# Attention scores computed a second time, keys by queries, in place of transposed probabilities

## The chip, the cores and the metric

The kernel runs on one core of one Trainium2 chip. A core has engines that run side by side, each with its own in-order stream of instructions: PE (TensorE, matmuls into PSUM), DVE (VectorE), ACT (ScalarE, activations and copies), POOL (GpSimd, which does not touch PSUM here) and SP (SyncE, which here only starts DMAs). The metric is the time of one execution on the device in microseconds (us), lower is better. The time before is the median of three runs.

## What is computed

One transformer block over 2048 tokens of width 1024, all in 32-bit floats: a LayerNorm, 32 heads of attention in four segments of 512 tokens with a memory carried from one segment to the next, an output projection with a residual, two LayerNorms, and an MLP of width 3584. The change lies in the softmax attention inside a segment. Cut to that (H = 32 heads, Dh = 32, L = 512):

```python
h = x + A(layernorm(x))                  # attention
h2 = h + B(layernorm(h))                 # MLP with its own LayerNorm
# inside A, for each segment s:
logits = einsum("bhqd,bhkd->bhqk", qs, ks) * Dh ** -0.5 + mask   # -1e9 above the diagonal
p = softmax(logits, axis=-1)
a_dot = einsum("bhqk,bhkd->bhqd", p, vs)
a_mem = (phi(qs) @ M) / (phi(qs) @ z + 1e-6)
o = g * a_mem + (1.0 - g) * a_dot        # g = sigmoid(beta), one value a head
```

## The kernel before, in words

Every 32-bit matrix is split into a high part that TensorE's fast 32-bit mode keeps exactly and a low rest, and a product is the sum of high by high, high by low and low by high.

The sequence is done in two halves of 1024 tokens. A half is: attention, output projection (`wo_first`, `wo_second`), LayerNorms, MLP. In attention eight groups `g` of four heads run over the half's two segments `sl`; one group and segment is a unit, so there are 32 units and 128 heads (one head of one segment counts as one head here).

`dense(g, sl, ...)` makes a unit's keys, queries and values: three projections (`kps`, `qps`, `vps`) of eight steps each, a step being three matmuls of 512 columns (`mm3`, lines 115 to 117). It builds the stacks: for each head, `ks` holds the key's high, low and high part in 96 rows, `qs` the query's high, high and low part, so that one 96-row product gives the exact score. Twelve DMAs a unit fill each kind of stack on SP's queue (line 377); a kind has five buffers. `vs` holds the values by tokens, high and low side by side (64 columns).

Heads of the unit before run between the projection steps of the unit that is projected. `slot` issues one head's work in six steps by the table `PLAN`; the head in its first pass is `cur`, the one before it `p1`, the one before that `p2`, so a head's work is spread over up to three slots. `interleave` takes one step of `heads` after each projection step, so a unit's 24 projection steps hold four slots. The plan's letters are: `q` score product of 128 queries by their keys with the row minimum of minus the score on DVE (line 542) and the exponential on ACT with the row sum (line 550); `n` normalization by sum and gate on POOL (line 557); `t` transposes of the probabilities on PE (line 573) and the cast to the high part on ACT (line 575); `s` the low part on DVE (line 580); `a` output products on PE (line 593), keys block by block; `o` the sum of the two value parts on DVE (line 604), the memory's part on POOL and the store or the split for the output projection.

Small matmuls of the memory (`one_small`) are slipped between the heads' matmuls. PSUM's eight banks are shared by tag: three for projections and small matmuls (`d`), two for scores (`qk`), two for transposes (`pt`), one for outputs (`av`).

The order in the program is only a priority. The framework plans when the kernel is built: it takes for each engine and queue the earliest instruction in the program's order that it expects to be ready, by its own estimates of durations, and puts in every wait. That plan is fixed: on the chip each engine then works in that order. Manual dependencies (`add_manual_dep`) force an order where they stand.

At the end of a half the last unit's heads run between the steps of `wo_first`, which multiplies the first segment's outputs; its steps for the last group wait for that group's output.

Of the kernel before, what the change touches and what calls it, by code (L numbers as in the profile page):

```python
# [17 lines left out]
P = 128  # L18
# [12 lines left out]
PLAN = ('q1 S2', 'q0 n0 a0', 'q2 t0 a1', 'q3 n2 s0 o', 't1', 's1 t2')  # L31
SCALE = DH ** -0.5
EPS = 1e-5
DEN_EPS = 1e-6
# [9 lines left out]
def build(tc, x, wq, wk, wv, wo, beta, w1, b1, w2, b2, out):  # L44
# [11 lines left out]
    hsel = const.tile([P, 76], F32, name="hsel")[:, 0:4]  # L56
# [11 lines left out]
    def constants():  # L68
# [3 lines left out]
        nc.scalar.activation(gate[:, 1, :], gate[:, 0, :], AF.Identity, scale=-1.0, bias=1.0)  # L72
        pb = ps_dense("pb")
# [5 lines left out]
    mz_dram = dram.tile([P, NG * 132 + 96], F32, name="mz_dram")  # L79
    o_dram = [dram.tile([NG, P, 512], F32, name=f"o_dram{s}") for s in range(4)]  # L80
# [251 lines left out]
    def attention_pool(half):  # L332
# [5 lines left out]
        acts["mz"] = ab.tile([P, NG * 132 + 96], F32, name="MZ")  # L338
        if half == 0:
            nc.gpsimd.memset(acts["mz"], 0.0)  # L340
        else:
            nc.sync.dma_start(acts["mz"], mz_dram)

    def attention(half, first):
# [27 lines left out]
        def stack(a, b, name, order):  # L372
            out = []
            for j in range(4):
                st = ab.tile([96, 512], F32R, tag=name, name=name, bufs=5)
# [5 lines left out]
        small = []  # L381

# [19 lines left out]
        def dense(g, sl, ws, u):  # L402
# [59 lines left out]
            vs = ab.tile([P, 16, 64], F32R, name="vs", bufs=2)  # L462
            u["vs"] = vs
# [66 lines left out]
        offs = [0, 128, 384, 768]  # L530
        koff = [0, 512, 1024, 896]

        def qk(st, i):
            u, j = st["u"], st["j"]
            if "pr" not in st:
                st["pr"] = ab.tile([P, 1280], F32, name="pr", bufs=2)
                st["mx"] = ab.tile([P, 32], F32, name="mx", bufs=4)
                st["nm"] = ab.tile([P, 32], F32, name="nm", bufs=4)
            n = P * (i + 1)
            pqk = psum.tile([P, 512], F32, tag="qk", name="pqk", bufs=2)  # L540
            nc.tensor.matmul(pqk[:, :n], u["qs"][j][:, i * P:(i + 1) * P], u["ks"][j][:, 0:n], start=True, stop=True)  # L541
            nc.vector.tensor_tensor_reduce(  # L542
                out=st["pr"][:, offs[i]:offs[i] + n], in0=pqk[:, :n], in1=mask[:, 512 - n:512],
                op0=ALU.add, op1=ALU.min, scale=-SCALE, scalar=3.0e38, accum_out=st["mx"][:, i:i + 1])
            soft(st, i)

        def soft(st, i):
            pr, mx = st["pr"], st["mx"]
            pi = pr[:, offs[i]:offs[i] + P * (i + 1)]
            nc.scalar.activation(pi, pi, AF.Exp, bias=mx[:, i:i + 1], scale=-1.0, accum_out=mx[:, 4 + i:5 + i])  # L550

        def norm(st, i):
            pr, mx, nm, j, g = st["pr"], st["mx"], st["nm"], st["j"], st["u"]["g"]
            nc.vector.reciprocal(nm[:, 4 + i:6 + i], mx[:, 4 + i:6 + i])  # L554
            for k in (i, i + 1):
                pi = pr[:, offs[k]:offs[k] + P * (k + 1)]
                nc.gpsimd.tensor_scalar(pi, pi, nm[:, 4 + k:5 + k], gate[:, 1, 4 * g + j:4 * g + j + 1],  # L557
                                        op0=ALU.mult, op1=ALU.mult)

        def ptr(st, n):  # L560
            grp = ((0,), (1, 3), (2,))[n]
            if n == 0:
                st["pth"] = ab.tile([P, 1280], F32R, name="pth", bufs=2)
                st["ptl"] = ab.tile([P, 1280], F32R, name="ptl", bufs=2)
            pr, pth, ptl = st["pr"], st["pth"], st["ptl"]
            ppt = psum.tile([P, 512], F32, tag="pt", name="ppt", bufs=2)
            base = koff[grp[0]]
            w = 0
            for jk in grp:
                for i in range(jk, 4):  # L570
                    one_small()
                    o = koff[jk] - base + (i - jk) * P
# [9 lines left out]
        def av(st, n):  # L582
            u, j = st["u"], st["j"]
            if n == 0:
                st["po"] = psum.tile([P, 512], F32, tag="av", name="po", bufs=1)[0:64, :]
# [858 lines left out]
```

## Time and profile before

| what | value |
|---|---|
| time, median of three runs | 2301.37 us (2301.26 to 2301.75) |
| span of the profiled execution | 2296.2 us |
| median of the runs minus that span | 5.2 us |
| PE busy | 2270.4 us, 99% of the span |
| DVE, ACT, POOL busy | 67%, 53%, 48% of the span |
| granted TensorE clock | 1.000 |
| attention with heads running, both halves | about 36 to 520 us and 920 to 1425 us |

The profiled execution has no time of its own in the runs; its span, from its first to its last instruction, is 5.2 us under the median of the runs, and that much lies around it.

How to read it: a group of instructions is given by source line, engine, operation, output and inputs; then its count, its busy time and the mean duration of one in ns; then how long the engine had been idle just before such instructions and what ended that idle time. Durations of matmuls overlap, so they do not add. `SPq` and `ACTq` are DMA issues on the queues of SP and ACT; what is issued from ACT's queue stands in ACT's own order.

### The profile page before, as it was taken

Reading aid. Unit: us, or ns where it says so; the run is one execution under the profiler, and the core shown is the slowest. Engines: PE = TensorE matmul, PEld = TensorE weight load, DVE = VectorE, ACT = ScalarE, POOL = GpSimd, SP = SyncE. Lnnn points to the kernel's source line nnn. Section 1 sums busy time; section 2 is a strip of 40 time slices with the busy share of each in tenths; the row PEclk is TensorE's granted clock in tenths of the full one; section 3 lists DMA queues with packets and bytes.
Section 4 is the critical chain, followed back from the end, with each engine's and each line's share of the span. In section 5 each row is a group of like instructions: output and inputs, shape, how many; then the busy total and the mean of one; then the engine's idle time right before and its main releaser. Section 6 shows DMA issues by size and latency. Waiting matters only on the chain.

```text
span 2296.2 us, 35279 instructions
## 1 busy us (share of the span) xinstructions
PE 2270.4 (99%) x11769; PEld 1890.8 (82%) x11769; DVE 1540.3 (67%) x3173; ACT 1225.0 (53%) x2549; POOL 1092.4 (48%) x1134
## 2 busy tenths in 40 slices
PE   8999999999999999999999999999999999999999
PEld 6888888878888888888888887888888888888887
DVE  6777777776655565777777777565566766577563
ACT  6777777775453445777777776363344223322221
POOL 5545555555244442555555556253445554155430
PEclk9999999999999999999999999999999999999999
DMA  6333333345465654433333344466667976476762
GB/s 190 92 85 91 93 89 85 87 120 182 139 204 172 188 165 142 113 91 86 85 87 88 87 111 140 156 211 175 176 188 263 345 243 216 159 253 221 249 234 90
DMA packets 322719, 355.36 MB, mean 155 GB/s; under 512 B 26190, under 2 KB 218730, under 8 KB 322538
## 3 DMA queue, kind: packets, MB, share of 16 engines
q1 hardware_dynamic: 259370, 316.40, 45.4%
q10 hardware_dynamic: 63168, 36.71, 5.3%
q8 instruction: 93, 1.52, 0.3%
q14 instruction: 88, 0.72, 0.1%
HBM read 226.59 MB, written 76.09 MB: 132 GB/s over the span
## 4 chain that ended last, share of the span: by engine, by line
PE 91%; ACT 3%; POOL 2%; DVE 2%; issue 1%; DMA 1%; ACTq 0%; SPq 0%; POOLq 0%; DVEq 0%
PE po L1278 22%; PE bps L882 9%; PE cps L882 7%; PE dps L882 6%; PE po L593 6%; PE ppt L573 6%; PE pqk L541 3%; PE vps L116 2%; PE vps L115 2%; PE kps L115 2%; PE kps L116 2%; PE vps L117 2%; PE kps L117 2%; PE pwo L117 2%; PE pwo L116 2%; PE pwo L115 2%
## 5 line engine op out<-in xcount | busy, mean ns | idle before, releaser
L557 POOL TENSOR_SCALAR pr<-pr,nm,gate 128x128 f32<-128x128 f32 (+3 forms) x512 | 322.6, 639 | 345.9 <-DVE nm L554 260.0
L550 ACT ACTIVATE pr<-pr,mx 128x256 f32<-128x256 f32 (+3 forms) x512 | 287.6, 562 | 161.9 <-DVE mx L542 158.2
L580 DVE TENSOR_TENSOR ptl<-ppt,pth 128x512 fp32r<-128x512 f32 (+1 forms) x384 | 227.2, 599 | 86.2 <-ACT pth L575 82.0
L542 DVE CUSTOM_DVE_ANT_0 pr<-pqk,mask 128x256 f32<-128x256 f32 (+3 forms) x512 | 243.3, 484 | 46.5 <-PE pqk L541 43.7
L573 PE MATMUL ppt<-ident,pr 128*128 128x128 f32 x1280 | 223.6, 277 | 2.1 <-POOL pr L557 1.4
L575 ACT CAST pth<-ppt 128x512 fp32r<-128x512 f32 (+1 forms) x384 | 194.2, 517 | 39.0 <-PE ppt L573 33.1
L1288 DVE TENSOR_TENSOR c<-c,po 128x512 f32<-128x512 f32 x160 | 105.4, 683 | 143.1 <-PE po L1278 135.5
L573 PEld LDWEIGHTS ppt<-ident,pr 128*128 128x128 f32 x1280 | 164.6, 140 | 32.5 <-POOL pr L557 2.6
L541 PE MATMUL pqk<-ks,qs 96*128 96x256 f32 (+3 forms) x512 | 161.3, 315 | 0.0
L92 POOL TENSOR_TENSOR wl<-wr,wh 128x1024 fp32r<-128x1024 f32 x52 | 124.5, 2393 | 70.8 <-PE pqk L541 27.6
L593 PE MATMUL po<-pth,vs 128*64 128x512 f32 (+3 forms) x512 | 155.4, 326 | 0.3 <-ACT pth L575 0.2
L593 PE MATMUL po<-ptl,vs 128*64 128x512 f32 (+3 forms) x512 | 153.9, 310 | 1.3 <-DVE ptl L580 1.2
L1278 PE MATMUL po<-w2h,zh 128*128 128x512 f32 x378 | 121.1, 390 | 0.8 <-DVE zh L1218 0.4
L1135 POOL TENSOR_TENSOR w2r<-w2r 128x512 f32<-128x512 f32 x54 | 85.4, 1593 | 72.0 <-DVE c L1288 36.9
L541 PEld LDWEIGHTS pqk<-ks,qs 96*128 96x128 f32 x512 | 96.2, 188 | 21.5
L994 POOL TENSOR_TENSOR s<-r 128x512 f32<-128x512 f32 x28 | 43.6, 1559 | 143.4 <-DVE sa L1010 87.1
L882 PE MATMUL bps<-zh,sb 128*128 128x512 f32 x336 | 111.0, 391 | 0.0
L882 PE MATMUL bps<-zh,sa 128*128 128x512 f32 x336 | 110.8, 390 | 0.0
L115 PE MATMUL vps<-yh,wh 128*128 128x512 f32 x256 | 109.4, 427 | 0.9 <-DVE MZ L497 0.9
L115 PE MATMUL kps<-yh,wh 128*128 128x512 f32 (+1 forms) x264 | 110.1, 417 | 0.0
L115 PE MATMUL qps<-yh,wh 128*128 128x512 f32 x256 | 106.8, 417 | 0.0
L1278 PE MATMUL po<-w2h,hl 128*128 128x512 f32 x322 | 103.2, 390 | 0.5 <-POOL hl L1218 0.3
(241 smaller groups left out, 6657.1 us busy)
## 6 DMA issues: line engine op xcount, KB each, us to landing
hr<-h_dram SPq DMA_DIRECT2D x112, 448.0 KB, 5.4
w2r<-in_B_w SPq DMA_DIRECT2D x122, 256.0 KB, 4.4
r<-in_B_w SPq DMA_DIRECT2D x56, 512.0 KB, 4.5
h_dram<-ht ACTq DMA_DIRECT2D x84, 256.0 KB, 3.7
ks<-kh SPq DMA_DIRECT2D x256, 64.0 KB, 2.0
qs<-qh SPq DMA_DIRECT2D x256, 64.0 KB, 2.0
wr<-in_A_wo SPq DMA_DIRECT2D x32, 512.0 KB, 4.0
wx<-in_B_w SPq DMA_DIRECT2D x56, 256.0 KB, 3.5
```

Of the source, the lines that this page charges most:

```text
L115: nc.tensor.matmul(ps, ah, bh, start=first, stop=False)
L116: nc.tensor.matmul(ps, ah, bl, start=False, stop=False)
L541: nc.tensor.matmul(pqk[:, :n], u["qs"][j][:, i * P:(i + 1) * P], u["ks"][j][:, 0:n], start=True, stop=True)
L542: nc.vector.tensor_tensor_reduce(out=st["pr"][:, offs[i]:offs[i] + n], in0=pqk[:, :n], in1=mask[:, 512 - n:512], op0=ALU.add, op1=ALU.min, ...
L550: nc.scalar.activation(pi, pi, AF.Exp, bias=mx[:, i:i + 1], scale=-1.0, accum_out=mx[:, 4 + i:5 + i])
L557: nc.gpsimd.tensor_scalar(pi, pi, nm[:, 4 + k:5 + k], gate[:, 1, 4 * g + j:4 * g + j + 1], op0=ALU.mult, op1=ALU.mult)
L573: nc.tensor.transpose(ppt[:, o:o + P], pr[:, offs[i] + jk * P:offs[i] + (jk + 1) * P], ident)
L575: acts["pth"] = n, nc.scalar.copy(pth[:, base:base + w], ppt[:, :w])
L580: nc.vector.tensor_tensor(o, x0, x1, op=ALU.subtract)
L593: nc.tensor.matmul(po[:, P * jk:], v, st[part][:, koff[jk]:koff[jk] + w], start=(jk, part) == (0, "pth"), stop=(jk, part) == (2, "ptl"))
L882: nc.tensor.matmul(ps, x_[:, c, :], y_[:, c, :], start=first and c == 0 and n == 0, stop=last and c == 3 and n == 2, skip_group_check=True)
L1278: nc.tensor.matmul(ps, x_[:, k], y_[k], start=opens and k == 0 and i == 0, stop=closes and k == self.KP - 1 and i == 2, skip_group_check=True)
```

## The change

The transposes of the probabilities, their normalization before the output product and the sums of the exponential go. In their place:

- The row minimum of minus the unscaled score still comes from the first score product (`qk`); the masked scores are written back into PSUM and not used further.
- `halves` splits the minima of a head's four query blocks into a high and a low part on POOL; `rows` turns these eight columns into rows with one transpose, copies them to SBUF on ACT and sends them with two DMAs on ACT's queue into rows 96 and 97 of the head's query stack. The key stacks hold ones in these rows, set once in eight buffers that are used in turn. The query stacks keep their five buffers.
- `turned` multiplies key blocks by queries over 98 rows, so the product is the score minus its row maximum, already with keys on the partitions; ACT takes the exponential, POOL clears the triangle above the diagonal.
- `cast` makes the high part on ACT and the low part on DVE (on POOL for the third group).
- The values get a column of ones (column 64), so that row 64 of the output product holds the sums (`av`, 65 rows).
- `av_out` sends the sum row of each head by DMA into 32 partitions; after the fourth head it takes reciprocals, multiplies by one minus the gate, stores the weights to DRAM, loads them back spread over 32 partitions a head, and multiplies the output.
- `PLAN` becomes the table below; small matmuls are slipped in at nine places a head, not at seventeen. The unit's output tile moves to the pool of LayerNorm tiles, and the loads of `x` for the first output blocks are ordered behind one of the output copies.

```diff
-PLAN = ('q1 S2', 'q0 n0 a0', 'q2 t0 a1', 'q3 n2 s0 o', 't1', 's1 t2')
+PLAN = ('q1 r c1', 'q2 c2', 'q0 a0', 'q3 a1 b0', 'b1 a2', 'b2 m c0 o')
...
+        acts["ks"] = [ab.tile([98, 512], F32R, name=f"ks{i}") for i in range(KB)]
+        acts["vs"] = [ab.tile([P, 16, 72], F32R, name=f"vs{i}") for i in range(2)]
+        for t in acts["ks"]:
+            nc.gpsimd.memset(raw(t[96:98, :]), 1.0)
+        for t in acts["vs"]:
+            nc.gpsimd.memset(raw(t[:, :, 64:65]), 1.0)
...
             nc.vector.tensor_tensor_reduce(
-                out=st["pr"][:, offs[i]:offs[i] + n], in0=pqk[:, :n], in1=mask[:, 512 - n:512],
-                op0=ALU.add, op1=ALU.min, scale=-SCALE, scalar=3.0e38, accum_out=st["mx"][:, i:i + 1])
-            soft(st, i)
...
+                out=pqk[:, :n], in0=pqk[:, :n], in1=mask[:, 512 - n:512],
+                op0=ALU.add, op1=ALU.min, scale=-1.0, scalar=3.0e38, accum_out=st["mx"][:, i:i + 1])
+
+        def halves(st):
+            mm = st["mm"] = ab.tile([P, 32], F32R, name="mm", bufs=2)
+            nc.gpsimd.tensor_copy(mm[:, 0:4], st["mx"][:, 0:4])
+            nc.gpsimd.tensor_tensor(mm[:, 4:8], st["mx"][:, 0:4], raw(mm[:, 0:4]), op=ALU.subtract)
+
+        def rows(st):
+            pm = psum.tile([P, 512], F32, tag="pt", name="pmr", bufs=2)
+            one_small()
+            nc.tensor.transpose(pm[0:8, 0:P], raw(st["mm"][:, 0:8]), ident)
+            mr = ab.tile([P, P], F32, name="mr", bufs=1)[0:8, :]
+            nc.scalar.copy(mr, pm[0:8, 0:P])
+            q = st["u"]["qs"][st["j"]]
+            for r in range(2):
+                nc.scalar.dma_start(raw(q[96 + r:97 + r, :]), mr[4 * r:4 * r + 4, :])
+
+        def turned(st, n):
...
+            for jk in groups[n]:
+                c = P * (4 - jk)
+                w += c
+                nc.tensor.matmul(ps[:, koff[jk]:koff[jk] + c], u["ks"][j][:, jk * P:(jk + 1) * P], u["qs"][j][:, jk * P:],
+                                 start=True, stop=True)
+            pe = st["pe", n] = ab.tile([P, 512], F32, tag="pe", name="pe", bufs=3)
+            nc.scalar.activation(pe[:, :w], ps[:, :w], AF.Exp, scale=SCALE)
+            d = pe[:, 0:P * len(groups[n])].rearrange("p (a b) -> p a b", b=P)
+            nc.gpsimd.affine_select(d, d, pattern=[[0, len(groups[n])], [1, P]], compare_op=ALU.is_ge, fill=0.0, base=0,
+                                    channel_multiplier=-1)
+
+        def cast(st, n):
...
+            acts["pth"] = n, nc.scalar.copy(st["pth", n][:, :w], pe)
+            (nc.gpsimd if n == 2 else nc.vector).tensor_tensor(st["ptl", n][:, :w], pe, raw(st["pth", n][:, :w]),
+                                                              op=ALU.subtract)
...
+            nc.scalar.copy(sm[32 * j:32 * j + 1, :], po[64:65, :])
+            nc.sync.dma_start(rq[b, :], sm[32 * j:32 * j + 1, :])
+            op = nc.scalar.copy(ot[b, :], po[32:64, :])
...
             if j == 3:
+                g = u["g"]
+                nc.vector.reciprocal(rq, rq)
+                nc.gpsimd.tensor_scalar(rq, rq, gatec[:, g:g + 1], None, op0=ALU.mult)
+                rd = r_dram[turns["v"] % 2]
+                nc.sync.dma_start(rd.rearrange("j (e n) -> (j e) n", n=16), rq)
+                rr = u["rr"]
+                for k in range(4):
+                    nc.sync.dma_start(rr[32 * k:32 * k + 32, :], rd[k:k + 1, :].to_broadcast([32, 512]))
+                nc.gpsimd.tensor_tensor(ot, ot, rr, op=ALU.mult)
...
-            ops = {"q": (cur, qk), "n": (cur, norm), "N": (p1, norm), "t": (p1, ptr), "s": (p1, sub), "S": (p2, sub),
-                   "a": (p2, av), "o": (p2, av_out)}
+            ops = {"q": (cur, qk), "m": (cur, halves), "r": (p1, rows), "b": (p1, turned), "c0": (p1, cast),
+                   "c": (p2, cast), "a": (p2, av), "o": (p2, av_out)}
...
-            nc.sync.dma_start(hts[t], x[0, r0:r0 + P, :])
+            op = nc.sync.dma_start(hts[t], x[0, r0:r0 + P, :])
+            if sl == 0:
+                tc.add_manual_dep(op.ins, acts["ot"].ins.name, NOSYNC, reason="program order")
```

More of the change, by code (lines that the diff above doesn't have):

```diff
@@ L545, in qk @@
-            soft(st, i)
[L547 to L567, printed above, removed]
-            w = 0
[L569 to L572, printed above, removed]
-                    nc.tensor.transpose(ppt[:, o:o + P], pr[:, offs[i] + jk * P:offs[i] + (jk + 1) * P], ident)
-                    w += P
-            acts["pth"] = n, nc.scalar.copy(pth[:, base:base + w], ppt[:, :w])
-            st["sub", n] = (ptl[:, base:base + w], ppt[:, :w], raw(pth[:, base:base + w]))
```

77 lines of the change are left out of this document (48 added, 29 removed).

## The prediction

> **What bounds the kernel now.** I read the page first, then two stretches of the attention by engine, then the order of time inside one head.
>
> ```profile
> span 2296.2 us, 35279 instructions
> ...
> PE 2270.4 (99%) x11769; PEld 1890.8 (82%) x11769; DVE 1540.3 (67%) x3173; ACT 1225.0 (53%) x2549; POOL 1092.4 (48%) x1134
> ...
> PE 91%; ACT 3%; POOL 2%; DVE 2%; issue 1%; DMA 1%; ACTq 0%; SPq 0%; POOLq 0%; DVEq 0%
> ```
> ```profile
> 1000.00:1300.00 300.00, 300.00 (x1838) 254.37 (x1837) 226.81 (x678) 219.93 (x559) 167.39 (x226) 1.00 0.34 87
> ```
> ```profile
> L573 PE MATMUL ppt<-ident,pr 128*128 128x128 f32 x390 | 68.0, 277 | 0.0
> ```
>
> The first fence is the page (span, engines, the chain that ended last); the second a stretch of attention by engine (PE, PEld, DVE, ACT, POOL, granted clock); the third one group in that stretch. PE carries 91% of the chain and is busy for all 300 us, at full clock; DVE stands at 76%, ACT at 73%, POOL at 56%. The 390 transposes are 10 a head, so 39 heads in 300 us: 7.69 us a head, of which a head's own steps are only part, since projections run between them. Busy time doesn't price a matmul, because durations overlap; the distance from one start to the next does.
>
> ```profile
> 401.53 0.22 PE L541 MATMUL pqk<-ks,qs 96*128 96x128 f32 x1
> 401.59 0.39 PE L593 MATMUL po<-pth,vs 128*64 128x512 f32 x1
> ...
> 403.09 0.34 PE L541 MATMUL pqk<-ks,qs 96*128 96x384 f32 x1
> 403.27 0.60 PE L573 MATMUL ppt<-ident,pr 128*128 128x128 f32 x4
> 403.62 0.30 PE L593 MATMUL po<-pth,vs 128*64 128x128 f32 x1
> 403.77 0.23 PE L593 MATMUL po<-ptl,vs 128*64 128x128 f32 x1
> ...
> 404.76 0.39 PE L541 MATMUL pqk<-ks,qs 96*128 96x512 f32 x1
> 404.99 0.40 PE L115 MATMUL vps<-yh,wh 128*128 128x512 f32 x1
> 405.22 0.40 PE L116 MATMUL vps<-yl,wh 128*128 128x512 f32 x1
> ...
> 405.69 0.60 PE L573 MATMUL ppt<-ident,pr 128*128 128x128 f32 x4
> 406.04 0.48 PE L115 MATMUL vps<-yh,wh 128*128 128x512 f32 x1
> 406.36 0.40 PE L116 MATMUL vps<-yl,wh 128*128 128x512 f32 x1
> ```
>
> Here a score product of 512 columns holds PE 0.23 us (404.76 to 404.99), of 384 0.18, of 128 0.06; 256 are taken as half of 512, 0.12. A product over 128 rows holds it as long (404.99 to 405.22), so 98 rows in place of 96 cost nothing. Four transposes and the product behind them take 405.69 to 406.36, 0.67; less that product's 0.23 it is 0.44, or 0.11 a transpose.
>
> **The change on PE, a head.** Removed: 10 transposes, 1.10 us. Added: four products by keys, 0.23 + 0.18 + 0.12 + 0.06 = 0.59; one transpose of the eight columns of maxima, 0.11; and a small exposed load where the 128-column product stands ahead of a small output product: between 0 and the 0.09 by which 403.62 to 403.77 exceeds 0.06, taken as 0.04. The 65th output row changes no column count. Net 1.10 - 0.74 = 0.36 us a head; the 1280 transposes of the page are 128 heads: **46 us off PE**.
>
> **The other engines.** They cost nothing while they stay below PE, which is their cover; without it, these loads would show.
>
> ```profile
> L557 POOL TENSOR_SCALAR pr<-pr,nm,gate 128x128 f32<-128x128 f32 (+3 forms) x512 | 322.6, 639 | 345.9 <-DVE nm L554 260.0
> L550 ACT ACTIVATE pr<-pr,mx 128x256 f32<-128x256 f32 (+3 forms) x512 | 287.6, 562 | 161.9 <-DVE mx L542 158.2
> ...
> L575 ACT CAST pth<-ppt 128x512 fp32r<-128x512 f32 (+1 forms) x384 | 194.2, 517 | 39.0 <-PE ppt L573 33.1
> ```
> ```profile
> L550 ACT ACTIVATION_READ_ACCUMULATOR pr<-pr,mx 128x1 f32 x512 | 96.4, 188 | 0.0
> ...
> L575 ACT CAST pth<-ppt 128x256 fp32r<-128x256 f32 x128 | 49.2, 385 | 10.1 <-PE ppt L573 10.0
> ...
> L363 ACT ACTIVATE e<-qps 128x512 f32<-128x512 f32 x24 | 14.6, 607 | 1.5 <-DVE ql L428 1.5
> ...
> L75 ACT COPY b1c<-pb 128x28 f32<-128x28 f32 x1 | 0.2, 189 | 0.0
> ```
> ```profile
> 649.21 0.58 ACT L952 COPY p<-cps 128x512 f32<-128x512 f32 x1
> 649.82 0.33 ACTq L953 DMA_DIRECT2D p_dram<-p  x1
> 650.18 0.62 ACT L830 CAST zh<-t2t 128x512 fp32r<-128x512 f32 x1 [0.40 <-ACT p L952]
> ```
> ```profile
> qs<-qh SPq DMA_DIRECT2D x256, 64.0 KB, 2.0
> ...
> o_dram<-ot SPq DMA_DIRECT2D x28, 256.0 KB, 2.3
> orr<-o_dram SPq DMA_DIRECT2D x28, 256.0 KB, 3.2
> ```
>
> ACT loses four exponentials with their reads of the sum, (287.6 + 96.4) / 128 = 3.0 us a head, and gets three without sums: 0.61 + 0.61 + 0.39 = 1.6. The three casts stay, 194.2 / 128 = 1.5; their source is now SBUF, which I cost at nothing. New are the copy of the turned maxima (0.19 to 0.39), the copy of the sum row (0.58, as at 649.21) and two DMA issues of at least 0.33 each, which the engine waits out (idle 0.40 at 650.18). So +0.1 us a head by the low ends, +0.9 if issues go as slowly as SP's stack issues (0.59, below). From 73% of 7.69 us, 5.6, to between 5.7 and 6.5 in 7.4 us: 77 to 88%. It stays behind PE, with longer queues.
>
> DVE loses two reciprocals and the 256-wide subtraction, and its two 512-wide subtractions now read SBUF twice: no more load. POOL loses 322.6 / 128 = 2.5 us and gets two splits of four columns, three triangle cuts and a 256-wide subtraction:
>
> ```profile
> L449 POOL TENSOR_TENSOR pql<-pq,pqh 128x512 fp32r<-128x512 f32 x24 | 31.0, 1290 | 27.4 <-ACT pqh L445 26.1 <-DMA qs<-ql 1.3
> ...
> L446 POOL CAST mzh<-MZ 128x132 fp32r<-128x132 f32 x24 | 7.4, 307 | 2.7 <-DMA MZ<-mz_dram 1.7
> ...
> L336 POOL TENSOR_SCALAR_AFFINE_SELECT mask<-mask 128x128 f32<-128x128 f32 x2 | 0.6, 292 | 0.1
> ```
>
> Some 2 x 0.31 for the splits, 4 x 0.29 for the cuts, 0.65 (half of 1.29) for the subtraction and a quarter of a unit's 0.31 + 1.29 for the weights: 2.8, so POOL goes from 56% to some 62%.
>
> **The new wait.** The second product of a head can't start until the rows of its maxima have landed in its stack. In the plan the turn (r) stands in step 0 and the product (b0) in step 3. PE has between them nine projection matmuls (9 x 0.23), q2, q0, q3 (0.47), and the output products a0, a1 (2 x 0.23 + 2 x 0.18): 3.4 us, some 3.6 with the small matmuls. The chain needs: the turn's own 0.27 (277 ns above); ACT's queue, 0 to one 0.59 operation; the copy, 0.19 to 0.39; two issues, 0.33 to 0.59 each, the second's landing 2.0 after its start. With 0.1 of gaps that is 2.9 to 3.9, against 3.6: from 0.7 early to 0.3 late. PE queues every later matmul behind b0, projections too, so lateness is paid in full. I take 0.1 us a head on average, because both ends lie close about the cover: **13 us**, with ends 0 and 0.3 x 128 = 38.
>
> **SP.** A unit (four heads) adds nine issues (four sum rows, one weight store, four broadcasts) to 24 stack issues:
>
> ```profile
> 402.72 0.59 SPq L377 DMA_DIRECT2D qs<-ql  x1
> ```
> ```profile
> SPq L377 <- ACT pr L550: 221.2, 39, 10.9
> ```
>
> That is 33 x 0.59 = 19 us of a unit's 30. Its longest waits (39 of them) are stack loads held for a free stack; eight key stacks end those for ks, while qs, still five, is held one slot longer. Queued behind such a hold are the sum rows, weights and later stacks; a query stack is needed a slot or more later, so I cost this at nothing.
>
> **Ends.** A unit's output now goes through a sum row (2.0), a store (2.3), a broadcast load (up to 3.2) and a product (1.29), about 9 us longer. Only the first segment's last unit is awaited, in two halves: 0 to 18 us; PE meanwhile has the last unit's heads and other output blocks, so I take 3. At the start eight memsets stand ahead of the first LayerNorm on POOL:
>
> ```profile
> 0.86 0.53 POOL L335 MEMSET mask<- 128x512 f32 x1
> ...
> 1.92 1.06 POOL L340 MEMSET MZ<- 128x1152 f32 x1
> 5.55 0.19 POOL L129 TENSOR_SCALAR v<-mv 128x1 f32<-128x1 f32 x1 [2.58 <-DVE mv L126]
> ```
>
> 2.98 + 8 x 0.53 = 7.2 against 5.55: 0 to 1.7 late, taken as 1. The x loads of the output stage move to the end of attention; heads cover them.
>
> **Sum.** -46 + 13 + 3 + 1 = -29. The span 2296.2 becomes 2267; the median of the runs, 2301.4, lies 5.2 above the span, so 2272.
>
> **Rivals.** *The rows are late* (other sign). Same place, but ACT's queue is two operations deep and small DMAs land later: 0.6 us a head. (0.6 - 0.36) x 128 + 4 = +35: 2336. It decides from 0.33 us a head. For it: ACT at 77 to 88% in one fixed order, four operations of step 5 ahead of the copy. Against: the same ACT leaves PE no wait now.
>
> *The split of the maxima queues on POOL behind the last triangle cut.* Then r waits for b2 (0.28), its exponential (0.39), the cut (0.29) and the split (2 x 0.31), 1.6 us, where PE has only one projection step, b2 and q1, 0.9: 0.7 late, so (0.7 + 0.1 - 0.36) x 128 + 4 = +60: 2361. Against: the maxima are there a step earlier, and the planner issues by readiness.
>
> *DVE and POOL hold each other up.* DVE's subtraction with both inputs in SBUF is slow in another stage:
>
> ```profile
> L1144 DVE TENSOR_TENSOR w2l<-w2r,w2h 128x512 fp32r<-128x512 f32 x63 | 69.1, 1110 | 7.8 <-ACT w2h L1143 7.3
> ...
> L932 DVE TENSOR_TENSOR wl<-wx,wh 128x512 fp32r<-128x512 f32 x8 | 5.7, 715 | 20.3 <-ACT wh L926 20.3
> ```
>
> 1.11 against 0.72 us for one form. If 0.2 us a head of that reaches a0, the sum is -29 + 26: 2298. Against: a0 stands three steps behind its cast. [...]
>
> *No wait at all*: -46 + 1: 2256.
>
> **How the numbers follow.** Likeliest 2272 (2258 to 2292), 0.45; no wait 0.09; hold-up 0.12 (0.04 faster, 0.06 same, 0.02 slower); rows late 0.23; split late 0.11. Faster by over 0.2% (4.6 us, about what can be told from no change here) is 0.58, same 0.06, slower 0.36. 2250 to 2345 leaves out the late split and the tails.
>
> **What would show it.** Right: no transposes of probabilities, second products about 0.59 us a head by start distances, a head at 7.4 us, waits of those products on the row DMA under 0.3. Wrong: PE waiting on a q stack's rows or on the split of maxima, PE's busy share well under 99%, ACT above 90%.

## The result, and the profile after

The changed kernel takes 2479.22 us (median of four runs, 2475.35 to 2483.68) against 2301.32 for the kernel before beside it: 1.0774 times as long, 95% interval 1.0759 to 1.0789, so 178 us slower where 29 us faster were predicted. The lines of its page that answer the first fence of the prediction:

```profile
span 2481.7 us, 34905 instructions
...
PE 2309.3 (93%) x11129; PEld 1854.7 (75%) x11129; DVE 1519.9 (61%) x2822; ACT 1207.8 (49%) x2165; POOL 1137.2 (46%) x1475
...
PE 60%; ACT 10%; POOL 7%; DVE 7%; issue 7%; DMA 6%; SPq 2%; ACTq 1%; POOLq 0%; DVEq 0%
```

No engine got fuller: DVE, ACT and POOL all show a smaller share of the span than before. PE went from 91% to 60% of the chain that ended last, and what it lost is spread over ACT, POOL, DVE, DMA and issue. A chain that changes engine that often is a relay, not a saturated engine. PE's idle time is 2481.7 - 2309.3 = 172.4 us, where it was 2296.2 - 2270.4 = 25.8: 147 of the 185 us by which the span grew. The other 39 are longer busy time, part of it at a lower clock (mean 0.989 against 1.000, below).

A stretch of steady attention after the change, by engine (the same columns as in the prediction: PE, PEld, DVE, ACT, POOL, granted clock), and the groups of instructions in it:

```profile
1150.00:1450.00 300.00, 273.27 (x1481) 215.67 (x1479) 197.26 (x513) 191.11 (x395) 160.70 (x290) 1.00 0.34 85
```
```profile
L596 ACT CAST pth<-pe 128x512 fp32r<-128x512 f32 (+1 forms) x105 | 56.7, 549 | 42.9 <-POOL pe L588 36.7 <-ACT pth L596 6.1
L597 DVE TENSOR_TENSOR ptl<-pe,pth 128x512 fp32r<-128x512 f32 x70 | 54.0, 773 | 30.1 <-ACT pth L596 28.5
L586 ACT ACTIVATE pe<-pst 128x512 f32<-128x512 f32 (+1 forms) x105 | 53.7, 529 | 30.5 <-PE pst L583 28.8 <-DVE ql L445 1.0
...
L588 POOL TENSOR_SCALAR_AFFINE_SELECT pe<-pe 128x128 f32<-128x128 f32 (+1 forms) x106 | 38.1, 360 | 61.7 <-ACT pe L586 60.2 <-PE pqk L556 0.6 <-DMA qs<-ql 0.5
...
L569 PE MATMUL pmr<-ident,mm 128*8 128x128 f32 x35 | 9.5, 273 | 0.0
```

There are 35 turns (L569), so 35 heads in 300 us: 8.57 us a head, where 7.69 were needed before and 7.4 were expected. Per head, ACT is busy 191.11 / 35 = 5.46 us (5.64 before), DVE 5.64 (5.82), POOL 4.59 (4.29). PE stands idle (300 - 273.27) / 35 = 0.76 us a head; before it stood idle for none of the 300 us. The groups form a ring of waits. POOL's cut waits for ACT's exponential (60.2 us), ACT's cast waits for POOL's cut (36.7 us, 1.05 us a head), DVE's subtraction waits for ACT's cast (28.5 us), and ACT's exponential waits for PE's second product (28.8 us).

What PE waits for, over the whole execution (total us, times, longest):

```profile
PE pqk L556 <- DVE mx L557: 32.9, 48, 2.1
PE qps L121 <- DVE om L501: 25.3, 20, 3.9
PE pst L583 <- DMA qs<-mr: 17.8, 22, 2.5
PE po L611 <- DVE ot L628: 17.6, 28, 1.2
```

Only the third row is the wait that the prediction spoke of. The first, second and fourth are PSUM banks that DVE has not yet read out: of scores, of the dense tag (`d`), of head outputs.

One passage shows how DVE comes to be late. The timeline of the changed kernel (start, duration, engine, line, operation; in brackets the idle time before it and what ended it):

```profile
1236.73 1.22 ACTq L574 DMA_DIRECT2D qs<-mr  x2
...
1237.99 0.59 ACT L444 CAST qh<-qps 128x512 fp32r<-128x512 f32 x1 [1.29 <-DMA qs<-mr]
...
1238.49 2.38 POOL L98 TENSOR_TENSOR wl<-wr,wh 128x1024 fp32r<-128x1024 f32 x1 [1.60 <-PE pmm L412]
...
1239.46 0.47 PE L583 MATMUL pst<-qs,ks 98*128 98x512 f32 x1 [0.89 <-DMA qs<-mr]
...
1239.96 0.60 ACT L586 ACTIVATE pe<-pst 128x512 f32<-128x512 f32 x1 [1.38 <-PE pst L583]
...
1240.46 0.40 PE L583 MATMUL pst<-qs,ks 98*128 98x384 f32 x2
1240.70 0.23 PE L611 MATMUL po<-pth,vs 128*65 128x128 f32 x1
...
1241.76 0.28 PE L583 MATMUL pst<-qs,ks 98*128 98x256 f32 x1
...
1241.88 0.39 PE L121 MATMUL vps<-yh,wh 128*128 128x512 f32 x1
...
1242.57 0.28 PE L556 MATMUL pqk<-ks,qs 96*128 96x256 f32 x1
1242.58 0.29 POOL L588 TENSOR_SCALAR_AFFINE_SELECT pe<-pe 128x128 f32<-128x128 f32 x1
1242.68 0.27 PE L569 MATMUL pmr<-ident,mm 128*8 128x128 f32 x1
1242.71 0.48 PE L121 MATMUL vps<-yh,wh 128*128 128x512 f32 x1
...
1242.90 0.62 ACT L596 CAST pth<-pe 128x512 fp32r<-128x512 f32 x1 [0.87 <-POOL pe L588]
1243.03 0.40 PE L122 MATMUL vps<-yl,wh 128*128 128x512 f32 x1
...
1243.43 0.38 ACT L586 ACTIVATE pe<-pst 128x256 f32<-128x256 f32 x1
...
1243.56 0.69 DVE L597 TENSOR_TENSOR ptl<-pe,pth 128x512 fp32r<-128x512 f32 x1 [1.26 <-ACT pth L596]
...
1244.16 0.43 DVE L557 CUSTOM_DVE_ANT_0 pqk<-pqk,mask 128x256 f32<-128x256 f32 x1
```

PE waits 0.89 us for the rows (1239.46). The exponential is done at 1240.56, but POOL is in a weight split of 2.38 us with more of its fixed order behind it, and makes the cut at 1242.58, 2.0 us later. ACT stands 0.87 us at the cast for it; queued behind that cast is the exponential of a product that PE had started at 1241.76 (1243.43). DVE stands 1.26 us for the cast, and queued behind its subtraction are the minima of the next scores (1244.16), which free a score bank whose product PE had started at 1242.57. Nobody is short of time; each engine waits at the head of its own line while work that is ready stands behind.

Where in the kernel the time went. The first and last key projection and the first matmul of the MLP, in both halves, show it; before, then after:

```profile
L115 PE MATMUL kps<-yh,wh x136: 278/398/562, 14.9 to 477.7; 128*128 128x512 f32 x120, 128*128 128x256 f32 x16
...
L115 PE MATMUL kps<-yh,wh x128: 387/398/481, 889.4 to 1349.4; 128*128 128x512 f32 x128
...
L882 PE MATMUL cps<-zh,wh x112: 387/389/481, 615.1 to 694.4; 128*128 128x512 f32 x112
...
L882 PE MATMUL cps<-zh,wh x112: 387/389/481, 1485.8 to 1565.1; 128*128 128x512 f32 x112
```
```profile
L121 PE MATMUL kps<-yh,wh x136: 274/396/562, 15.7 to 543.4; 128*128 128x512 f32 x120, 128*128 128x256 f32 x16
...
L121 PE MATMUL kps<-yh,wh x128: 387/396/487, 988.0 to 1499.4; 128*128 128x512 f32 x128
...
L923 PE MATMUL cps<-zh,wh x112: 387/389/481, 713.7 to 793.0; 128*128 128x512 f32 x112
...
L923 PE MATMUL cps<-zh,wh x112: 387/389/481, 1669.7 to 1749.0; 128*128 128x512 f32 x112
```

From first to last key projection ("the stage") the halves took 462.8 and 460.0 us, and now take 527.7 and 511.4: +116 us. From there to the MLP ("the ends": the last heads, the output projection and a LayerNorm) they took 137.4 and 136.4, and now 170.3 twice: +67. The rest of the kernel is unchanged to 2 us. The experiments are read by the same two sums.

### The profile page after: what moved, and what is told of

It reads as the page before. It is cut to its first block, busy times and chain, and to the rows that moved or that the text cites. A ratio compares the mean times of both kernels' runs of the same rounds, so it can differ in the third digit from the quotient of the medians.

```text
span 2481.7 us, 34905 instructions
## 1 busy us (share of the span) xinstructions
PE 2309.3 (93%) x11129; PEld 1854.7 (75%) x11129; DVE 1519.9 (61%) x2822; ACT 1207.8 (49%) x2165; POOL 1137.2 (46%) x1475
## 4 chain that ended last, share of the span: by engine, by line
PE 60%; ACT 10%; POOL 7%; DVE 7%; issue 7%; DMA 6%; SPq 2%; ACTq 1%; POOLq 0%; DVEq 0%
PE po L1319 20%; PE bps L923 9%; PE cps L923 6%; PE dps L923 6%; PE po L611 3%; ACT pe L586 2%; PE pqk L556 2%; POOL wl L98 1%; POOL pe L588 1%; PE pwo L122 1%; PE pwo L123 1%; PE pst L583 1%; PE pwo L121 1%; ACT pth L596 1%; DVE ptl L597 1%
## 5 line engine op out<-in xcount | busy, mean ns | idle before, releaser
L557 DVE CUSTOM_DVE_ANT_0 pqk<-pqk,mask 128x256 f32<-128x256 f32 (+3 forms) x512 | 248.2, 500 | 85.6 <-PE pqk L556 79.7
L597 DVE TENSOR_TENSOR ptl<-pe,pth 128x512 fp32r<-128x512 f32 x256 | 205.1, 803 | 155.9 <-ACT pth L596 152.3
L596 ACT CAST pth<-pe 128x512 fp32r<-128x512 f32 (+1 forms) x384 | 208.5, 548 | 161.8 <-POOL pe L588 126.6
L586 ACT ACTIVATE pe<-pst 128x512 f32<-128x512 f32 (+1 forms) x384 | 196.7, 528 | 128.4 <-PE pst L583 122.3
L588 POOL TENSOR_SCALAR_AFFINE_SELECT pe<-pe 128x128 f32<-128x128 f32 (+1 forms) x384 | 142.1, 374 | 254.2 <-ACT pe L586 250.0
L556 PE MATMUL pqk<-ks,qs 96*128 96x256 f32 (+3 forms) x512 | 172.4, 338 | 33.5 <-DVE mx L557 32.9
L611 PE MATMUL po<-pth,vs 128*65 128x512 f32 (+3 forms) x512 | 153.7, 316 | 22.3 <-DVE ot L628 17.6
L611 PE MATMUL po<-ptl,vs 128*65 128x512 f32 (+3 forms) x512 | 157.3, 314 | 10.8 <-DVE ptl L597 5.4
L597 POOL TENSOR_TENSOR ptl<-pe,pth 128x256 fp32r<-128x256 f32 x128 | 102.6, 802 | 134.8 <-ACT pth L596 119.4
L583 PE MATMUL pst<-qs,ks 98*128 98x512 f32 (+3 forms) x512 | 135.7, 325 | 22.0 <-DMA qs<-mr 17.8
L583 PEld LDWEIGHTS pst<-qs,ks 98*128 98x128 f32 x512 | 95.8, 189 | 56.9 <-issue 13.6
L628 DVE TENSOR_TENSOR ot<-po,ot 32x512 f32<-32x512 f32 x120 | 81.7, 681 | 51.9 <-ACT ot L625 49.2
```

The source lines that it names most:

```text
L556: nc.tensor.matmul(pqk[:, :n], u["qs"][j][0:96, i * P:(i + 1) * P], u["ks"][j][0:96, 0:n], start=True, stop=True)
L557: nc.vector.tensor_tensor_reduce(out=pqk[:, :n], in0=pqk[:, :n], in1=mask[:, 512 - n:512], op0=ALU.add, op1=ALU.min, scale=-1.0, scalar=3. ...
L583: nc.tensor.matmul(ps[:, koff[jk]:koff[jk] + c], u["ks"][j][:, jk * P:(jk + 1) * P], u["qs"][j][:, jk * P:], start=True, stop=True)
L586: nc.scalar.activation(pe[:, :w], ps[:, :w], AF.Exp, scale=SCALE)
L588: nc.gpsimd.affine_select(d, d, pattern=[[0, len(groups[n])], [1, P]], compare_op=ALU.is_ge, fill=0.0, base=0, channel_multiplier=-1)
L596: acts["pth"] = n, nc.scalar.copy(st["pth", n][:, :w], pe)
```

## The experiments

The theory after the result: the scores' new way (PE, exponential on ACT, cut on POOL, cast on ACT, subtraction on DVE, PE) and the weights' new way (ACT, SP, DVE, POOL, SP to DRAM and back, POOL) cross fixed-order engines so often that each holds up what is queued behind it. The first rival: the rows of maxima are late. Further rivals: one single operation (the cut, SP's issues, ACT's second copy) is to blame. Every run was timed beside the kernel before, whose median there was between 2301.2 and 2302.9 us. Every version is also planned anew, so an edit changes more than the part it takes out: already in e1, which only changes how many rows a product reads, DVE works in another order than in the changed kernel. The intervals below hold what differs from run to run, not what a new plan adds; after e1's rise of 18 us (below), a difference of 10 to 20 us between two versions can't be put down to the edit alone.

**Taking parts out.**

```diff
 # e1: the rows are made and sent, but the second product reads only 96 rows
-... u["ks"][j][:, jk * P:(jk + 1) * P], u["qs"][j][:, jk * P:],
+... u["ks"][j][0:96, jk * P:(jk + 1) * P], u["qs"][j][0:96, jk * P:],
 # e2: no cut
-            nc.gpsimd.affine_select(d, d, ...)
 # e3: no weights
-            nc.scalar.copy(sm[32 * j:32 * j + 1, :], po[64:65, :])
-            nc.sync.dma_start(rq[b, :], sm[32 * j:32 * j + 1, :])
-                nc.vector.reciprocal(rq, rq)
...
-                nc.gpsimd.tensor_tensor(ot, ot, rr, op=ALU.mult)
 # e4: e1, e2 and e3 together
 # e8: e2 and e3 together
 # e5: e4, and no split, turn, copy and sending of rows
-PLAN = ('q1 r c1', 'q2 c2', 'q0 a0', 'q3 a1 b0', 'b1 a2', 'b2 m c0 o')
+PLAN = ('q1 c1', 'q2 c2', 'q0 a0', 'q3 a1 b0', 'b1 a2', 'b2 c0 o')
```

> The second product reads 96 rows of the stacks instead of 98, so nothing waits for the two rows of maxima; they are still split, turned, copied and sent (the maximum is not subtracted). Theory of the late rows: most of the 117 us lost while projections run goes, 2479 becomes 2350 to 2390. Theory of the relay (the second scores pass ACT, POOL, ACT and DVE one after another, and each engine stands in its fixed order until the one before is done): the row transfers only account for the 18 us that PE shows on them, 2455 to 2475. Theory of the weights (sum rows through DMA): no more than 20 us either.

> The triangle cut on POOL is left out (384 instructions; keys above the diagonal inside a diagonal block count in the output), so the cast on ACT no longer waits for POOL. Theory of the relay: ACT's 162 us of idle before the casts, 127 of them put down to POOL, and DVE's behind them shrink, and the time falls by 60 to 120 us, to 2360 to 2420. Theory of the late rows: within 15 us of 2479. Theory of the weights: within 15 us.

> The sums are still made by the ones, but the copy of the sum row, its DMA, the reciprocal, the store, the broadcast loads and the product with the weights are left out (outputs are not divided by their sums and not gated). Theory of the weights: SP no longer stands behind sum rows, and the 67 us lost in the two stretches after the last projection mostly go, with part of the wait for the one output bank: 2390 to 2420. Theory of the relay: ACT also loses 0.58 us a head, so 15 to 40 us. Theory of the late rows: under 20 us.

> The three together: rows unread, no cut, no weights. What the removed transposes should have brought shows here if these three waits are all that stood against it: 2255 to 2300 then. If 2330 or more is left, a fourth cause is open (buffers of PSUM, ACT's load of copies, or the plan itself).

> As the run of all three, and the maxima are neither split nor turned, copied or sent. What is left of the change is the second product in place of the transposes. If the run of all three (2299) was held by the split of the maxima, on which its PE stands 9 us in the profile and more in start distances (the product of 256 columns ahead of the turn holds PE 0.29 us instead of 0.12), this one gives 2250 to 2275, and the 46 us of PE work show. If the second product itself gains nothing, it stays within 10 us of 2299.

> Cut and weights left out, rows read as in the changed kernel. Against the run of all three (2299) this prices the wait for the row transfers alone once the other two are gone. Theory of the late rows in its weaker form (they bind as soon as the rest does not): 2330 to 2360. If they never bind: 2295 to 2315. Sum of the two single removals: 2479 - 75 - 58 = 2346.

| kernel | us | ratio to before, 95% interval | stage against before | ends against before |
|---|---|---|---|---|
| changed kernel | 2479.2 | 1.0759 to 1.0789 | +116 | +67 |
| e1, rows unread | 2496.9 | 1.0813 to 1.0876 | +142 | +56 |
| e3, no weights | 2421.1 | 1.0475 to 1.0556 | +102 | +24 |
| e2, no cut | 2404.4 | 1.0403 to 1.0484 | +53 | +49 |
| e8, neither | 2326.8 | 1.0073 to 1.0131 | +12 | +16 |
| e4, neither, rows unread | 2299.0 | 0.9972 to 0.9996 | -11 | +11 |
| e5, and no rows at all | 2269.7 | 0.9825 to 0.9883 | -33 | +4 |

Late rows alone are not the cause: when nobody waits for them (e1) the time does not fall, it rises by 18 us, which no expectation had allowed for. PE's waits in that run (first rows of the view):

```profile
PE pqk L556 <- DVE mx L557: 47.3, 80, 2.1
PE pmr L569 <- ACT pe L586: 21.9, 25, 3.3
```

The wait for the rows is gone and the same time, and more, is waited elsewhere: PE is idle for 179.7 us, against 172.4 in the changed kernel, and its mean clock is 0.983 against 0.989. Without the weights (e3) the wait for the rows, the first row of the view, even doubles:

```profile
PE pst L583 <- DMA qs<-mr: 33.6, 35, 2.4
```

The waits lie side by side, and one covers another; a wait's total in the list is not what its removal is worth. The cut is worth 75 us, the weights 58 (more than the 15 to 40 of the relay theory), both together 152. Only then do the rows count: 28 us when they are no longer waited for (e8 to e4), and 29 more when they are no longer made (e4 to e5). By the profiled executions' stretches the cut works on the stage (116.3 - 52.5 = 64 us, and 18 in the ends), the weights on the ends (66.8 - 23.5 = 43, and 14 in the stage).

With all of it gone, PE's share is back, and its saving can be seen (page of e5):

```profile
span 2268.7 us, 32459 instructions
...
PE 2223.7 (98%) x11001; PEld 1838.9 (81%) x11001; DVE 1512.6 (67%) x2790; ACT 1123.5 (50%) x1909; POOL 908.9 (40%) x771
```

**The cut: its wait, or its work on POOL?** In e6 POOL makes the same cut into a tile that nobody reads (values four columns narrower in storage make room for it), so the work stays and the wait goes.

```diff
-            nc.gpsimd.affine_select(d, d, ...)
+            aside = ab.tile([P, 256], F32, name="aside", bufs=1)[:, 0:P * len(groups[n])]
+            nc.gpsimd.affine_select(aside.rearrange("p (a b) -> p a b", b=P), d, ...)
```

> The cut is still made by POOL on every block, but into a tile that nobody reads (so the triangle stays in the output; the value tile is four columns narrower a block to make room). Load kept, wait gone. If ACT standing at the cast for POOL is what the cut costs: 2395 to 2420, as with the cut left out (2404). If POOL's load is what costs: 2465 to 2485. Theory of the late rows: 2479.

It took 2424.9 us (ratio 1.0493 to 1.0563): 54 of the cut's 75 us are the wait, the other 21 go with POOL's work or with the new plan.

**What in the weights' way costs 58 us?** Three edits: the sum rows sent from ACT's queue instead of SP's (e7); the copy that frees the output ahead of the copy of the sums (f3); the sums copied and sent, but the group's reciprocal, store, broadcast loads and product left out (f1).

```diff
 # e7
-            nc.sync.dma_start(rq[b, :], sm[32 * j:32 * j + 1, :])
+            nc.scalar.dma_start(rq[b, :], sm[32 * j:32 * j + 1, :])
 # f3
+            op = nc.scalar.copy(ot[b, :], po[32:64, :])
             nc.scalar.copy(sm[32 * j:32 * j + 1, :], po[64:65, :])
             nc.sync.dma_start(rq[b, :], sm[32 * j:32 * j + 1, :])
-            op = nc.scalar.copy(ot[b, :], po[32:64, :])
 # f1
-                nc.vector.reciprocal(rq, rq)
...
-                nc.gpsimd.tensor_tensor(ot, ot, rr, op=ALU.mult)
```

> The sum rows' 128 DMAs are issued from ACT's queue, right behind the copy they wait for, instead of from SP's. All else as in the changed kernel. If SP standing at a sum row while weights and stacks wait behind it is what the weights cost (58 us by their removal): 2425 to 2450, most of it in the two stretches after the last projection. If ACT's time or the length of the output's own way counts: 2475 to 2500, since ACT gets 0.4 us a head more.

> Nothing left out: ACT copies the output's upper half ahead of the row of sums, so that DVE's addition, with the minima queued behind it, is released about 0.58 us earlier in each head. If the idle time of DVE ahead of its addition (49.2 us on ACT's copy, against 7.7 us without the weights) is what the weights' way costs, the time falls by 15 to 50 us, to 2430 to 2465. If what matters is when the output bank is free of both copies, or POOL's product, it stays at 2470 to 2485.

> Splits the 58 us of the weights' way: the row of sums is still copied by ACT and sent by SP for every head (128 of each), but the reciprocal, the store, the four broadcast loads and the product of a group (32 of each) are left out, so the outputs stay unweighed. If the cost lies per head (ACT's second copy ahead of the one that frees the output bank, and SP's issue), the time stays at 2460 to 2480. If it lies per group (POOL's product of 1.29 us, 32 times 1.29 = 41 us of POOL with cuts queued behind it, and DVE's reciprocal that stands for the sums' transfer, 10.9 us in 9 waits), it falls to 2425 to 2445.

e7 took 2502.9 us (1.0835 to 1.0898), 24 more: the ends gained 7 us (+59 against before), the stage lost 30. ACT now stands for four more issues a unit, which may be why; its issues of the rows take 0.58 us each in the changed kernel (median). f3 took 2473.7 (1.0711 to 1.0774), 5.5 less, and the intervals overlap. But DVE's addition was not released earlier: it now started behind the copy of the sums, as the row of DVE's waits says (`DVE ot L628 <- ACT sm L624: 45.7, 95, 2.8`, where the changed kernel has `DVE ot L628 <- ACT ot L625: 49.2, 98, 2.6`). So f3 shows that the order of ACT's two copies alone is worth next to nothing; what DVE's idle time ahead of its addition costs, it leaves open. f1 took 2448.9 (1.0604 to 1.0666), between its two expectations: about 30 of the 58 us are the group's way and 28 the heads'. Its place is clear: the ends fall from +67 to +34, the stage stays (+118). So the group's 30 us lie wholly in the ends, where no later heads run. Of the heads' 28 us about 10 lie there (+34 to +24) and 16 in the stage (+118 to +102).

The ends themselves, PE and the other engines in the first half's, before and after:

```profile
477.00:615.00 138.00, 134.01 (x693) 109.29 (x692) 93.06 (x192) 75.56 (x146) 64.57 (x75) 1.00 0.45 148
```
```profile
543.00:714.00 171.00, 148.18 (x653) 112.82 (x652) 96.77 (x173) 79.78 (x136) 74.14 (x101) 0.93 0.43 137
```

Of the 33 us, 19 are idle time (22.8 against 4.0) and about 10 are the clock, by the estimate 148 x 0.07. SP's queue there, in the changed kernel:

```profile
585.34 10.64 SPq L624 DMA_DIRECT2D rq<-sm  x2
596.13 3.26 SPq L741 DMA_DIRECT2D wr<-in_A_wo  x2
```

Two sum rows hold SP for 10.6 us, until ACT has copied the second of them (its copy ends at 595.45), and two loads of output-projection weights stand behind. e7 takes this hold off SP and gives ACT the issues; together that is worth some 7 us of the ends, not 33.

**Other versions of the change.** v1 only spaces the steps: casts and output products each stand one step later behind the second products, which stay where they were (so the first group's cast, too, moves into the slot after next). v2 copies outputs and sums in one ACT operation. v3 sends one row, the rounded maximum, without POOL's split. v4 is all three; f2 is v1 with v3; f4 is v1 without the cut.

```diff
 # v1
-PLAN = ('q1 r c1', 'q2 c2', 'q0 a0', 'q3 a1 b0', 'b1 a2', 'b2 m c0 o')
+PLAN = ('q1 r c0', 'q2 c1', 'q0 c2', 'q3 a0 b0', 'b1 a1', 'b2 m a2 o')
 # v2
-            op = nc.scalar.copy(ot[b, :], po[32:64, :])
-            nc.vector.tensor_tensor(ot[b, :], po[0:32, :], ot[b, :], op=ALU.add)
+            op = nc.scalar.copy(sm[0:65, :], po[0:65, :])
+            nc.sync.dma_start(rq[b, :], sm[64:65, :])
+            nc.vector.tensor_tensor(ot[b, :], po[0:32, :], sm[32:64, :], op=ALU.add)
 # v3
-            nc.tensor.transpose(pm[0:8, 0:P], raw(st["mm"][:, 0:8]), ident)
+            nc.tensor.transpose(pm[0:4, 0:P], st["mx"][:, 0:4], ident)
...
-            for r in range(2):
-                nc.scalar.dma_start(raw(q[96 + r:97 + r, :]), mr[4 * r:4 * r + 4, :])
+            nc.scalar.dma_start(raw(q[96:97, :]), raw(mr))
```

> Only the plan's table differs: each cast stands a step later after its product (three steps instead of two), the output products follow a step later, with the output in the same step as before. Work and results are those of the changed kernel. If ACT stands at the casts because the table leaves the cut too little time, this gives back a good part of the 54 to 75 us that the cut's wait costs: 2400 to 2445. If the planner's order has little to do with the table: within 20 us of 2479.

> One copy on ACT takes rows 0 to 64 of the output bank (sums and second value half together) where there were two, so ACT loses 0.58 us a head and the bank comes free that much earlier; the weights go their way as before. If the cost of the weights is ACT's second copy: 2425 to 2450, near the 2421 without weights. If it is the way through SP and DRAM: 2465 to 2485.

> Only the rounded maximum is sent, in one row with one DMA (the same rounding stands in numerator and sum, so it cancels); POOL's split and one DMA issue a head go, and PE turns DVE's maxima directly. The rows cost 28 us by their wait and 29 us by split, turn and issue in the kernel without cut and weights. If they cost as much here: 2420 to 2450. If the cut's and the weights' waits hide them, as the unread rows (2497) say: 2465 to 2500.

> Spaced table, one copy and one row together. If the three waits are independent ends of the same shortage of time in a fixed order, the gains add and more: 2340 to 2390; below 2301 only if the cut then costs nothing. If the plan is at fault as such, 2430 to 2480.

> The spaced order (2434.8) with the single row of the rounded maximum (2469.7 in the first order, 9 us less than the changed kernel), without the single copy of outputs and sums. If the single copy alone spoilt the version with all three (2503.7), this gives 2420 to 2435. If the row without POOL's split goes out too early or too late for the spaced order, 2440 to 2480.

> The spaced order (2434.8) with the cut left out, so that the sums and outputs take in keys after the query. In the first order the cut was worth 75 us (2404.4). If the spaced order gains because it gives the cut time, the two gains overlap and this gives 2395 to 2425. If they are independent, 2434.8 - 75 = 2360.

| kernel | us | ratio to before, 95% interval |
|---|---|---|
| v1, spaced | 2434.8 | 1.0547 to 1.0609 |
| v2, one copy | 2494.1 | 1.0804 to 1.0867 |
| v3, one row | 2469.7 | 1.0699 to 1.0761 |
| v4, all three | 2503.7 | 1.0846 to 1.0909 |
| f2, spaced with one row | 2444.8 | 1.0575 to 1.0659 |
| f4, spaced without the cut | 2391.4 | 1.0353 to 1.0417 |

The order alone is worth 44 us, with as many operations on each computing engine as before: part of the loss is where things stand in the lines. Its gain and the cut's overlap (f4 is 13 us under e2, not 44), and ACT's wait for the cut falls from 126.6 us in 164 cases to 58.2 in 84 over the whole execution; so the spaced order gains mostly by giving the cut time. The single row is worth 9 us in the first order, where the intervals just meet, and none in the spaced one (f2 is 10 over v1, and the intervals overlap; its expectation had blamed such a result on the row). The single copy takes 96 us of busy time off ACT (1111.8 against 1207.8) and makes the kernel slower by 15, outside both of its expectations; PE then waits longer for the output bank (first row of PE's waits in v2, and then one of ACT's):

```profile
PE po L611 <- DVE ot L627: 47.8, 52, 2.7
```
```profile
ACT sm L623 <- DMA rq<-sm: 29.2, 17, 3.0
```

The row of ACT's is a wait that the edit itself brought in. In the changed kernel each of the four heads has a row of its own in `sm`; in v2 all of them write the same 65 rows of its one buffer, so ACT's copy has to wait until SP has sent the sum row of the head before, and the output bank stays held meanwhile. In the changed kernel ACT's copy of the sums waits for nothing but PE. So v2 does not price ACT's second copy, as it was meant to, and what a single copy into buffers of its own would be worth was not run. Since f2 is without it, the single copy with its shared rows is also what spoils v4: 59 us between f2 and v4. About half of that, by the estimate in the last section, is the lower clock (0.974 and 0.977 in v4's two runs, 0.990 and 0.987 in f2's). v4, too, lies outside both of its expectations. No version that computes the whole block beats the kernel before; the best, v1, is 134 us behind.

## Why the prediction was wrong

**Off PE, 46 us.** The mechanism is right and the durations are nearly so. In the timeline above the products of 384 and 128 columns together take 0.24 us (1240.46 to 1240.70; 0.18 + 0.06 predicted), that of 256 takes 0.12 (1241.76 to 1241.88), and the turn 0.03 plus 0.09 by which the next product starts late (1242.68 to 1242.71 to 1243.03): 0.12 against 0.11. The exposed load, taken as 0.04, is not seen there: the small output product behind starts on time (1240.70). In e5, where rows and turn are absent too, the same prices give 0.36 + 0.11 = 0.47 a head, 60 us. PE's busy time fell by 2270.4 - 2223.7 = 47, and the kernel's time by 33, because PE's idle time rose from 25.8 to 45.0. About 13 us of PE's busy time are unaccounted for.

**"They cost nothing while they stay below PE, which is their cover."** This step failed, and with it the sign. Its premise held: ACT took 5.46 us a head, under the 5.7 to 6.5 foreseen (the prediction's own terms add up to +0.04 and +0.76 a head, so 6.5 should read 6.4), POOL exactly the 4.59 that 62% of 7.4 makes, DVE less than before. But a busy share says only whether an engine's whole work fits; it does not say when one operation comes to its turn. The cut was priced at 0.29 us of POOL's time. What it cost is a handover between ACT's exponential and ACT's cast, with ACT, then DVE, then PE's banks behind it: 75 us, 54 of them the wait alone (e6), with no engine but PE above 66% in the stage. The prediction asked what is queued behind a waiting instruction of the rows, of SP's loads and, in a rival, of the split; never of ACT's cast behind the cut.

**The new wait of the rows, 13 us (0 to 38).** PE's list shows 17.8 us. That this is near the estimate is chance: alone the wait is worth nothing (e1), behind the other waits it is worth 28 (e8 to e4), inside the bounds. The two issues took 1.22 us together (1236.73), 0.61 each, just above the upper bound of 0.59, and ACT stood 1.29 us for them. Making the rows costs another 29 us (e4 to e5), of which only the turn's 14 was in the sum.

**SP, nothing.** Off by some 7 us in the ends, as far as e7 shows (net of what the issues then cost ACT): the hold was looked for behind the stack loads, and it came behind the sum rows, with weight loads queued after them.

**Ends, 3 us (0 to 18).** 67 us, the second term that failed. The nine added microseconds of a unit's way were counted once, for the one unit that is awaited, and taken as nearly covered. In the ends PE has output blocks and the last heads, and both now hang on longer relays: 43 us went with the weights (e3), 33 of them with a group's reciprocal, store, loads and product (f1). Some 10 us in each half are the lower clock, by the estimate above. The last heads' own relay and rows make the rest, down to +4 in e5.

**Start, 1 us.** The memsets took 3.79 us, 0.47 each, and the first LayerNorm on POOL came at 7.19 instead of 5.55, 1.6 later:

```profile
2.10 3.79 POOL L348 MEMSET ks<- 2x512 f32 x8
...
7.19 0.19 POOL L135 TENSOR_SCALAR v<-mv 128x1 f32<-128x1 f32 x1
```

The first key projection starts 0.8 us later (15.7 against 14.9), near the term. But versions with the same memsets start it anywhere from 14.3 (v1, e7) to 16.5 (e6), so a term this small is not told from the plan's own spread.

**The rivals.** "The rows are late" named 2336 and the wrong cause. "The split of the maxima queues on POOL" looked at the right engine, but at the split instead of the cut. "DVE and POOL hold each other up" expected a slower subtraction; its 0.2 us a head on the way to a0, 26 us in all, was the author's estimate, and no run shows it. In the other stage, before, the 28 of the 63 subtractions of line 1144 (`w2l`) with no operation of POOL beside them took 0.68 to 0.69 us; of the other 35, 24 took over 1 us, up to 2.49. After the change the subtraction takes 0.773 us on DVE in the stretch, not 1.11: four of its 70 took 1.93 to 1.95, each beside two operations of POOL, and the 31 with none beside them at most 0.69. Over the whole execution PE's waits for it (`PE po L611 <- DVE ptl L597: 5.4, 10, 1.6`) come to 5.4 us; the 28.5 us that DVE stood idle for ACT's casts are another matter. All three looked for one late operation; the loss came from several that wait for each other. Of the signs of being wrong, PE's busy share well under 99% came true at 93%; ACT above 90% did not.

**What stays open.** Which of the heads' steps in the weights' way (copy, sending, or ACT's time) makes their 28 us, which neither f3 nor v2 could tell; how much of v2's loss is the wait for its shared rows; the 13 us of PE's busy time in e5. And the share of the fixed order in the loss is only bounded from below, by the 44 us of v1: other orders may do better.

## What to carry to other kernels

When a step is taken from the bounding engine and given to others, count the handovers between in-order engines that each unit of work now makes, and at each ask what is queued behind the waiting instruction; spare busy time on the receivers (DVE, ACT and POOL here at 61%, 49% and 46%) covers their work, not their waits. Price longer ways once more for the last units of a stage, where nothing later runs beside them. And don't read the worth of a wait from its total in a list: one whose removal alone gains nothing (e1, 18 us slower) can pay once those beside it are gone (28 us from e8 to e4).

## What the runs showed of the hardware

PE's clock fell to half after several short interruptions, which the prediction didn't allow for. In the ends of the changed kernel:

```profile
627.38 0.41 PE L611 MATMUL po<-pth,vs 128*65 128x512 f32 x1 [1.75 <-DVE otl L628]
...
630.66 0.39 PE L611 MATMUL po<-ptl,vs 128*65 128x384 f32 x1 [1.58 <-DVE ptl L597]
...
632.93 0.48 PE L611 MATMUL po<-ptl,vs 128*65 128x256 f32 x1 [0.96 <-POOL ptl L597]
633.21 0.63 PE L121 MATMUL pwo<-wh,oh 128*128 128x512 f32 x1
633.64 0.63 PE L122 MATMUL pwo<-wl,oh 128*128 128x512 f32 x1
...
638.76 0.47 PE L122 MATMUL pwo<-wl,oh 128*128 128x512 f32 x1
639.06 0.39 PE L123 MATMUL pwo<-wh,ol 128*128 128x512 f32 x1
639.29 0.39 PE L121 MATMUL pwo<-wh,oh 128*128 128x512 f32 x1
```

Three gaps of 1.75, 1.58 and 0.96 us within 7.3 us are followed by 5.5 us in which matmuls of 512 columns start every 0.43 us (granted clock 0.50), and then every 0.23 again (0.98). What in the gaps brings the clock down, and what brings it back, is not shown. Over the whole execution the mean clock was 0.989 against 1.000. That is some 25 us of the loss, by the estimate 2309 x 0.011 from PE's busy time, most of it in the ends, where the clock was 0.93 in both halves, against 1.00 in both stages. If the low clock always follows waits as it does here, these 25 us are waits paid a second time; over the whole execution that was not followed.
